# Attention state per head: row and column halves on TensorE, and float64 conversions spread over the chunks

## Chip, cores and metric

One kernel runs on one core of a Trainium2 chip. The metric is the time of an execution on the device, in microseconds (us); lower is better. Engines are called by the names of the profile: PE (TensorE, matmul), PEld (its weight loads), DVE (VectorE), ACT (ScalarE), POOL (GpSimd) and SP (SyncE, which here issues DMA transfers).

## What is computed

Three parts, one after the other. The kernel also takes the weights of the last part as float64 bits.

```python
# attention, B=4, H=8, S=768, D=48
for t in range(S):
    cur = einsum('bhd,bhde->bhde', u * k[t], v[t])
    y[t] = einsum('bhd,bhde->bhe', r[t], state + cur)
    state = w[:, None] * state + einsum('bhd,bhe->bhde', k[t], v[t])
# x: 3072 tokens x 384; routing of tokens to 8 experts, 384 tokens each
logits = x @ w_gate                       # tokens are handed out in order of the largest logit
out[mask_e] = relu(x[mask_e] @ w1[e]) @ w2[e]
# final mlp, 2048 wide
h = relu(x @ w_in);  result = (h * h) @ w_out
```

## The kernel before

**Attention.** The 768 steps of each of four batch entries are cut into six chunks of 128, so there are 24 chunks; chunk n belongs to batch n % 4 and is number c = n // 4 in it. Heads are worked on in four pairs i: the even head of a pair lies on partitions 0 to 47, the odd one on 64 to 111. For each chunk PE makes the products of r and k (`qk`, into `pA`), which DVE masks into `AM` (`am`); the gate columns of v (`vw`, into `pvw`); y in `pY` (`yout`), as the sum of the state's part, r times `T`, and the part inside the chunk, `AM` times v; and the chunk's own addition to the state (`kvm`, into `pkv`). The state `T[b]` is a block matrix of 112 x 112 per pair of heads, with zeros outside the two 48 x 56 blocks. So one matmul per pair takes both heads' state, and `tput` (DVE, from c = 1 on, ACT at c = 0) writes the two blocks apart, with the decayed state from `tdecay` (ACT) added. A chunk with c = 0 has no state's part, and the last four chunks make no state. `yev` adds `cv` to y, writes it to DRAM (`xs`, `xd`), and sums the gate logits into `L`.

The loop body works on three chunks at a time: qk of n + 1, the preparation of n + 2 (`prep`, `prep_cc` on DVE, `prep_ru`, `prep_ruk`, `prep_kk` on POOL), and yout, kvm, yev, tput of n. The loads of n + 4 (`rk`, `tk`) stand at its start in SP's queue. Within the attention every engine works in the order in which the code is written. Between these operations `R.step()` drops in steps of the routing of tokens, two a chunk, three from n = 16 and four from n = 20.

**Conversion.** The weights of the final mlp, `wi` and `wo`, 16 slabs each of 128 x 384, arrive as float64, 384 KB a slab. `Resident.fetch` asks for the slabs in turn (wi 0, wo 0, wi 1, ...), at most `ahead` of them at a time, into five buffers. `Resident.convert` cuts the work on a slab into pieces: c (L848), low (L849) and join (L845) on DVE put the float32 bits together; ACT then copies them into the high part (L830) and DVE subtracts it for the low part, the finish (L825). In the attention the finish is a piece of its own. In the first routing ACT's copy and the finish follow the join at once; in the first expert they follow one and two ticks later. `fill(n)` issues n pieces, alternating between two slabs.

**After the attention.** `close0` and `route(0)` choose the first expert's tokens: three rounds of comparing (`cm`), counting on PE (`misc`), `sat` and `n`, with one piece before sat and, in the first two rounds, one before n. Six more pieces and the loads of w1 and w2 follow. Then, for each of the eight experts, `expert` multiplies by w1 and w2 (split into `wh` by ACT and `wl` by DVE), and `mlp` by wi (`gmm`) and wo (`omm`). In the first expert three pieces are issued a tick, in its mlp two; before `gmm` of a slab its conversion has to be done. In this part PE and SP keep the order of the code, and a scheduler orders DVE, ACT and POOL.

Of the kernel before, what the change touches and what calls it, by code (L numbers as in the profile page):

```python
# [25 lines left out]
FT = mybir.dt.float32  # L26
# [4 lines left out]
AF = mybir.ActivationFunctionType  # L31
OP = mybir.AluOpType
AX = mybir.AxisListType

B, H, S, D = 4, 8, 768, 48
C = 128
NC = S // C
NCH = B * NC
# [7 lines left out]
NW, NRAW = 7, 5  # L46

def make_ident(nc, ident):
    nc.gpsimd.memset(ident, 1.0)
    nc.gpsimd.affine_select(ident, ident, pattern=[[1, 128]], compare_op=OP.is_equal, fill=0.0, base=0,  # L50
                            channel_multiplier=-1)


def attention(ctx, tc, a, R, L, RW, xd):
# [5 lines left out]
    V, G, A_, PE = nc.vector, nc.gpsimd, nc.scalar, nc.tensor  # L60
    att = ctx.enter_context(tc.tile_pool(name="att", bufs=1))
    ld = ctx.enter_context(tc.tile_pool(name="ld", bufs=5))
    wk = ctx.enter_context(tc.tile_pool(name="wk", bufs=2))
    ps = ctx.enter_context(tc.tile_pool(name="aps", bufs=1, space=bass.MemoryType.PSUM))
    p0, p1 = slice(0, 48), slice(64, 112)
    bh = lambda x: x.rearrange("p h e -> p (h e)")


    RK, TK = {}, {}
# [27 lines left out]
    ident = R.ident  # L97
    hm, hm2 = att.tile([128, 3, 8], FT, name="hm"), att.tile([128, 3, 8], FT, name="hm2")
    mask = att.tile([128, 128], FT, name="mask")
    T = [att.tile([112, 4, 112], FT, name=f"T{b}") for b in range(B)]  # L100
    kkb = [att.tile([128, 4, 112], FT, name=f"kk{j}") for j in range(2)]
    V.memset(Pw[:, :, :, 0:1], 1.0)
    V.memset(Qw[:, 1, :, 8:9], 1.0)
    warm = att.tile([1, 1], FT, name="warm")
    V.memset(dense, 1.0)
    V.memset(warm, 0.0)
    lead = ps.tile([128, 512], FT, name="pY", bufs=2)
    for _ in range(26):
        PE.matmul(lead, dense[:, :128], dense, start=True, stop=True)
    A_.activation(warm, warm, AF.Copy)  # L110
    for t in T[:2]:
        V.memset(t, 0.0)
    make_ident(nc, ident)
    for t in T[2:]:
        G.memset(t, 0.0)
    G.memset(mask, 1.0)
    G.affine_select(mask, mask, pattern=[[1, 128]], compare_op=OP.is_gt, fill=0.0, base=0, channel_multiplier=-1)
    G.iota(hm, pattern=[[128, 3], [-48, 8]], base=0, channel_multiplier=1, allow_small_or_imprecise_dtypes=True)
# [60 lines left out]
    t1s, cc, cv, pA, AM, pYs, tTs, pk = ({} for _ in range(8))  # L179

    def va(n):
        return TK[n][:, 768:1216].rearrange("p (h e) -> p h e", h=8)

    def prep(n):
        V.tensor_tensor(flat(RK[n]), flat(RK[n]), flat(WRK), op=OP.mult)
# [27 lines left out]

    def qk(n):
        AM[n] = wk.tile([128, 2, 4, 128], FT, name="AM")
        pA[n] = [ps.tile([128, 4, 128], FT, name="pA", bufs=4) for _ in range(2)]
        for i in range(4):
            for s, q in enumerate((p0, p1)):
                PE.matmul(pA[n][s][:, i], RK[n][q, 1, i], RK[n][q, 0, i], start=True, stop=True)  # L219

    def am(n, s):
        V.tensor_tensor(AM[n][:, s], pA[n][s], mask[:, None, :].to_broadcast([128, 4, 128]), op=OP.mult)

    def yout(n):
        c, b = divmod(n, B)


        p = ps.tile([128, 512], FT, name="pY", bufs=2)[:, :504].rearrange("p (h e) -> p h e", e=56)
        pYs[n] = p[:, :8]
        for i in range(4):  # L230
            if c:
                PE.matmul(bh(p[:, 2 * i:2 * i + 2, :]), RK[n][:, 0, i], T[b][:, i, :], start=True, stop=True,  # L232
                          skip_group_check=True)
            for s in range(2):
                h = 2 * i + s
                PE.matmul(p[:, h::8 - h], AM[n][:, s, i], TK[n][:, 768 + 56 * h:880 + 56 * h], start=not c,  # L236
                          stop=True, skip_group_check=True)

    def yev(n):

        c, b = divmod(n, B)
        j = b * NC + c
        xs = wk.tile([128, 8, 48], FT, name="xs")
        p = pYs[n]
        end = n == NCH - 1

        def put():
            if end:
                A_.activation(xs, p[:, :, :48], AF.Copy)
                G.tensor_tensor(xs, xs, cv[n][:, :, :48], op=OP.add)  # L250
            else:
                V.tensor_tensor(xs, p[:, :, :48], cv[n][:, :, :48], op=OP.add)
            nc.sync.dma_start(xd[j * 128:(j + 1) * 128], xs.rearrange("p h d -> p (h d)"))

        if not end:
            put()
        R.step(wide=False)
        lt = wk.tile([128, 8, 8], FT, name="lt")
        V.tensor_tensor(lt, p[:, :, 48:56], cv[n][:, :, 48:56], op=OP.add)  # L259
        R.step()  # L260
        V.tensor_reduce(L[:, j, :], lt.rearrange("p h e -> p e h"), axis=AX.X, op=OP.add)
        return put


    def tdecay(n):
        c, b = divmod(n, B)
        if c in (0, NC - 1):
            return
        t = tTs[n] = wk.tile([112, 4, 112], FT, name="tT")
        for i in range(4):  # L270
            A_.activation(t[:, i], T[b][:, i], AF.Copy, scale=W128[:, i])

    def kvm(n):
        if n // B == NC - 1:
            return
        p = pk[n] = ps.tile([112, 4, 112], FT, name="pkv")
        for i in range(4):
            PE.matmul(p[:, i, :], kkb[n % 2][:, i, :], bh(va(n)[:, 2 * i:2 * i + 2, :]), start=True, stop=True)  # L278

    def tput(n, s):  # L280
        c, b = divmod(n, B)
        if c == NC - 1:
            return
        x = slice(64 * s, 64 * s + 48), slice(None), slice(56 * s, 56 * s + 56)
        if c == 0:
            A_.activation(T[b][x], pk[n][x], AF.Copy)
        else:
            V.tensor_tensor(T[b][x], pk[n][x], tTs[n][x], op=OP.add)

    def keep_clock():  # L290
        t = ps.tile([128, 384], FT, name="pvw")
# [24 lines left out]
    for n in range(NCH):  # L316
        f1, f2 = n + 1 < NCH, n + 2 < NCH
        if n + 4 < NCH:
            load(n + 4)
        R.pace(n)  # L320
        if n == NCH - B:
            R.cnt0 = ps.tile([128, 4, 112], FT, name="pkv").rearrange("p a b -> p (a b)")
        tdecay(n)
        if f1:
            prep_cv(n + 1)
            qk(n + 1)
        if f2:
            prep(n + 2)
            prep_ru(n + 2)
            prep_ruk(n + 2)  # L330
            vw(n + 2)
        R.step(wide=False)
        if n + 1 < NCH - B:
            prep_kk(n + 1)
        if f1:
            am(n + 1, 0)
        R.step(wide=False)
        if f1:
            am(n + 1, 1)
        R.step(wide=False)  # L340
        yout(n)
        kvm(n)
        R.serve()
        if n >= NCH - B:
            R.flush()
        if n >= NCH - B - 1:
            keep_clock()
        if f2:
            prep_cc(n + 2)
        R.step()  # L350
        if n >= NCH - 2:
            RW.fill(5 if n == NCH - 2 else 3)
        last = yev(n)
        R.step()
        tput(n, 0)
        R.step()
        tput(n, 1)
        R.step()
        if n == NCH - 4:
            RW.ahead = NRAW  # L360
            RW.fetch()
    R.arrive(NC - 1, NC)
    RW.ahead = 2
    R.close0(ps.tile([128, 8, 8], FT, name="pvw").rearrange("p h e -> p (h e)"),
             ps.tile([128, 512], FT, name="pY", bufs=2), last)


class Routing:
# [844 lines left out]
```

## Time and profile before

| | us |
|---|---|
| runs: median (lowest to highest) of 3 | 837.24 (836.9 to 838.81) |
| profiled execution: its own time | 837.7 |
| span from the first to the last instruction | 836.0 |
| PE busy | 791.2 (95%) |
| DVE busy | 482.7 (58%) |
| ACT busy | 398.8 (48%) |
| POOL busy | 156.8 (19%) |
| mean granted clock of PE | 0.971 of full |

The profiled execution took 1.7 us more than its span. Shares of busy time are averages over parts with different limits, so what a change is worth is read from the part in which it is made. A line of the profile names the source line, the engine, the operation, and the tiles as out<-in.

### The profile page before, as it was taken

How to read it: one execution, taken by the hardware profiler on the slowest of the kernel's cores; microseconds unless marked ns; L12 is line 12 of the kernel's file. 1: busy time of each engine (PE TensorE's matmuls, PEld its weight loads, DVE VectorE, ACT ScalarE, POOL GpSimd, SP SyncE). 2: the span in 40 equal slices, each digit the busy share in tenths (PEclk: the TensorE clock that was granted, in tenths of full speed). 3: DMA queues.
4: the chain of work that ended last, by engine and by line, in shares of the span. 5: the costliest groups of instructions: out<-in, count | busy, mean ns of one | idle time of the engine just before them, and what ended most of it. 6: DMA issues, size and time to landing. Idle time of an engine off the chain costs nothing.

```text
span 836.0 us, 15218 instructions
## 1 busy us (share of the span) xinstructions
PE 791.2 (95%) x5572; PEld 757.1 (91%) x5572; DVE 482.7 (58%) x1271; ACT 398.8 (48%) x973; POOL 156.8 (19%) x256
## 2 busy tenths in 40 slices
PE   6999998397996999999999999999999999999996
PEld 4999997277886999999999999999999999999996
DVE  7789889888998457256616642674275234324211
ACT  2565553044555336444643554265426545544453
POOL 7876651020020101010101011000101010101001
PEclk9999999599997999999999999999999999999999
DMA  8988885164344204021302220131104023102000
GB/s 242 316 271 282 278 251 178 39 199 160 115 151 162 67 2 143 1 67 35 108 1 67 68 77 27 41 94 49 58 11 142 1 78 103 29 1 67 1 1 29
DMA packets 37515, 83.78 MB, mean 100 GB/s; under 512 B 5696, under 2 KB 25280, under 8 KB 37440
## 3 DMA queue, kind: packets, MB, share of 16 engines
q1 hardware_dynamic: 34368, 73.37, 28.1%
q0 software_dynamic: 3072, 9.44, 3.3%
q8 instruction: 44, 0.72, 0.4%
q14 instruction: 31, 0.25, 0.1%
HBM read 73.35 MB, written 9.44 MB: 99 GB/s over the span
## 4 chain that ended last, share of the span: by engine, by line
PE 83%; DVE 9%; DMA 4%; ACT 2%; issue 1%; SPq 1%; POOL 0%; POOLq 0%; DVEq 0%; ACTq 0%
PE acc L911 11%; PE ph L911 11%; PE acc L913 11%; PE acc L912 11%; PE ph L912 11%; PE ph L913 11%; PE pY L236 4%; PE pA L219 2%; PE pvw L211 2%; DMA raw<-in_w_dram 2%; PE pkv L278 2%; PE pY L232 2%; PE misc L652 2%; PE ph L980 2%; DMA tk<-in_tk_dram 1%; DVE raw L845 1%
## 5 line engine op out<-in xcount | busy, mean ns | idle before, releaser
L1025 DVE TENSOR_TENSOR al<-t,ah 128x384 fp32r<-128x384 f32 x128 | 71.3, 557 | 163.8 <-ACT t L1022 163.5
L1018 ACT ACTIVATE t<-ph 128x384 f32<-128x384 f32 x128 | 62.4, 488 | 144.2 <-PE ph L913 139.7
L908 DVE TENSOR_TENSOR wl<-raw,wh 128x384 fp32r<-128x384 f32 x128 | 69.7, 554 | 79.1 <-ACT wh L907 71.3
L911 PE MATMUL ph<-YH,wi 128*128 128x384 f32 x288 | 99.2, 344 | 6.4 <-ACT wi L830 6.4
L907 ACT ACTIVATE wh<-raw 128x384 fp32r<-128x384 f32 x128 | 65.1, 521 | 76.9 <-PE ph L912 28.3
L911 PE MATMUL acc<-wo,ah 128*128 128x384 f32 x288 | 98.3, 341 | 0.0
L913 PE MATMUL ph<-YH,wi 128*128 128x384 f32 x288 | 97.4, 338 | 0.3 <-DVE wi L825 0.2
L912 PE MATMUL ph<-YL,wi 128*128 128x384 f32 x288 | 97.3, 338 | 0.0
L912 PE MATMUL acc<-wo,ah 128*128 128x384 f32 x288 | 97.2, 338 | 0.0
L913 PE MATMUL acc<-wo,al 128*128 128x384 f32 x288 | 97.1, 337 | 0.0
L1040 POOL DMA_INDIRECT out_dram<-rows,idx x24 | 25.2, 1050 | 293.8 <-ACT rows L1038 289.5
L911 PE MATMUL acc<-ah,wh 128*128 128x384 f32 x192 | 67.1, 350 | 4.6 <-ACT wh L907 4.6
L1022 ACT ACTIVATE t<-t 128x384 f32<-128x384 f32 x128 | 67.1, 524 | 2.9
L1021 ACT ACTIVATE ah<-t 128x384 fp32r<-128x384 f32 x128 | 67.1, 524 | 2.8
L206 ACT ACTIVATE cv<-tk,cc 128x56 f32<-128x56 f32 x192 | 47.0, 328 | 41.4 <-DVE lt L259 41.4
L913 PE MATMUL acc<-ah,wl 128*128 128x384 f32 x192 | 65.3, 340 | 0.4 <-DVE wl L908 0.3
L912 PE MATMUL acc<-al,wh 128*128 128x384 f32 x192 | 65.1, 339 | 0.0
L911 PEld LDWEIGHTS ph<-YH,wi 128*128 128x128 f32 x288 | 54.5, 189 | 10.2 <-ACT wi L830 7.2
L236 PE MATMUL pY<-tk,AM 128*128 128x112 f32 x384 | 58.2, 281 | 0.0
L911 PE MATMUL ph<-XH,wh 128*128 128x384 f32 x168 | 57.0, 339 | 0.0
L913 PE MATMUL ph<-XH,wl 128*128 128x384 f32 x168 | 56.2, 335 | 0.0
L912 PE MATMUL ph<-XL,wh 128*128 128x384 f32 x168 | 56.1, 334 | 0.0
(241 smaller groups left out, 1808.7 us busy)
## 6 DMA issues: line engine op xcount, KB each, us to landing
raw<-in_w_dram SPq DMA_DIRECT2D x128, 192.0 KB, 2.5
tk<-in_tk_dram SPq DMA_DIRECT2D x24, 800.0 KB, 6.4
rk<-in_rk_dram SPq DMA_DIRECT2D x24, 448.0 KB, 6.2
raw<-in_wi_dram SPq DMA_DIRECT2D x16, 384.0 KB, 3.3
raw<-in_wo_dram SPq DMA_DIRECT2D x16, 384.0 KB, 3.2
xd<-xs SPq DMA_DIRECT2D x24, 192.0 KB, 2.2
rows<-xd,idx POOLq DMA_INDIRECT x24
out_dram<-rows,idx POOLq DMA_INDIRECT x24
```

What stands on the lines that cost most here:

```text
L206: A_.activation(cv[n][:, h], va(n)[:, h], AF.Copy, scale=cc[n][:, h:h + 1])
L236: PE.matmul(p[:, h::8 - h], AM[n][:, s, i], TK[n][:, 768 + 56 * h:880 + 56 * h], start=not c, stop=True, skip_group_check=True)
L907: A_.activation(hi, t, AF.Copy)
L908: (eng or V).tensor_tensor(lo, t, hi.bitcast(FT), op=OP.subtract)
L911: PE.matmul(o, l[0], r[0], start=first, stop=False)
L912: PE.matmul(o, l[0], r[1], start=False, stop=False)
L913: PE.matmul(o, l[1], r[0], start=False, stop=last)
L1018: A_.activation(t, o, AF.Relu)
L1021: A_.activation(gh, t, AF.Square)
L1022: A_.activation(t, t, AF.Square)
L1025: later(2, lambda: V.tensor_tensor(gl, t, gh.bitcast(FT), op=OP.subtract))
L1040: h = G.indirect_dma_start(out=out, out_offset=bass.IndirectOffsetOnAxis(ap=st[p]["idx"][:, i:i + 1], axis=0), in_=t, in_offset=None)
```

## The change

T becomes 56 wide: for each pair i the even head's 48 x 56 block on the lower partitions and the odd head's on the upper, with a fifth, zero entry behind the four. The state's part of y moves out of `yout` into a new `yinter`, called right after qk of the next chunk: eight matmuls of 48 rows, the even heads on the lower row half of the array and into one PSUM bank, the odd heads on the upper half and into another. Each writes 2 x 56 columns, of which the second 56 fall into an unused column block. `yout` then adds to what stands there. `kvm` makes each head's addition with a matmul of its own, the even head on columns 0 to 63 of the array, the odd one on 64 to 111, each with 56 columns of v. `tput` is one instruction. pY takes four PSUM banks instead of two, and pA two instead of four. Of the conversion, one piece is issued in each chunk from n = 9 to 21, four in chunk 22 and three in 23 (before: five and three, and none earlier); slabs are asked for from chunk 7 on. Access patterns of `yev` and the tiles of the lead matmuls and of `close0` follow from this. The diff, without these:

```diff
--- before.py
+++ after.py
...
-    T = [att.tile([112, 4, 112], FT, name=f"T{b}") for b in range(B)]
+    T = [att.tile([112, 5, 56], FT, name=f"T{b}") for b in range(B)]
...
-    lead = ps.tile([128, 512], FT, name="pY", bufs=2)
+    lead = ps.tile([128, 512], FT, name="pvw")
...
-    for t in T[:2]:
-        V.memset(t, 0.0)
     make_ident(nc, ident)
-    for t in T[2:]:
-        G.memset(t, 0.0)
+    for t in T:
+        G.memset(t[:, 4], 0.0)
...
     def qk(n):
         AM[n] = wk.tile([128, 2, 4, 128], FT, name="AM")
-        pA[n] = [ps.tile([128, 4, 128], FT, name="pA", bufs=4) for _ in range(2)]
+        pA[n] = [ps.tile([128, 4, 128], FT, name="pA", bufs=2) for _ in range(2)]
...
+    def yinter(n):
+        c, b = divmod(n, B)
+        p = ps.tile([128, 2, 512], FT, name="pY", bufs=2)[:, :, :504].rearrange("p s (i e) -> p s i e", e=56)
+        pYs[n] = p
+        for i in range(4 if c else 0):
+            for s, q in enumerate((p0, p1)):
+                PE.matmul(p[:, s, i::8 - i], RK[n][q, 0, i], T[b][q, i:i + 2], start=i == 0, stop=True, skip_group_check=True)
+
     def yout(n):
         c, b = divmod(n, B)
-        p = ps.tile([128, 512], FT, name="pY", bufs=2)[:, :504].rearrange("p (h e) -> p h e", e=56)
-        pYs[n] = p[:, :8]
+        p = pYs[n]
         for i in range(4):
-            if c:
-                PE.matmul(bh(p[:, 2 * i:2 * i + 2, :]), RK[n][:, 0, i], T[b][:, i, :], start=True, stop=True,
-                          skip_group_check=True)
             for s in range(2):
                 h = 2 * i + s
-                PE.matmul(p[:, h::8 - h], AM[n][:, s, i], TK[n][:, 768 + 56 * h:880 + 56 * h], start=not c,
-                          stop=True, skip_group_check=True)
+                PE.matmul(p[:, s, i::8 - i], AM[n][:, s, i], TK[n][:, 768 + 56 * h:880 + 56 * h],
+                          start=not c and i == 0, stop=True, skip_group_check=True)
...
     def tdecay(n):
...
-        t = tTs[n] = wk.tile([112, 4, 112], FT, name="tT")
+        t = tTs[n] = wk.tile([112, 4, 56], FT, name="tT")
...
     def kvm(n):
...
-        p = pk[n] = ps.tile([112, 4, 112], FT, name="pkv")
+        p = pk[n] = ps.tile([112, 4, 56], FT, name="pkv")
         for i in range(4):
-            PE.matmul(p[:, i, :], kkb[n % 2][:, i, :], bh(va(n)[:, 2 * i:2 * i + 2, :]), start=True, stop=True)
-
-    def tput(n, s):
+            for s, m in enumerate((64, 48)):
+                PE.matmul(p[64 * s:64 * s + m, i, :], kkb[n % 2][:, i, 64 * s:64 * s + m], va(n)[:, 2 * i + s, :],
+                          start=True, stop=True)
+
+    def tput(n):
...
         if c == 0:
-            A_.activation(T[b][x], pk[n][x], AF.Copy)
+            A_.activation(T[b][:, :4], pk[n], AF.Copy)
         else:
-            V.tensor_tensor(T[b][x], pk[n][x], tTs[n][x], op=OP.add)
+            V.tensor_tensor(T[b][:, :4], pk[n], tTs[n], op=OP.add)
...
             qk(n + 1)
+        yinter(n)
         if f2:
...
-        if n >= NCH - 2:
-            RW.fill(5 if n == NCH - 2 else 3)
+        if n >= 9:
+            RW.fill(1 if n < NCH - 2 else 4 if n < NCH - 1 else 3)
         last = yev(n)
         R.step()
-        tput(n, 0)
+        tput(n)
         R.step()
-        tput(n, 1)
         R.step()
-        if n == NCH - 4:
-            RW.ahead = NRAW
+        if n >= 7:
+            RW.ahead = 2 if n < NCH - 4 else NRAW
             RW.fetch()
```

On PE a chunk with a state reads, before (L219 is qk, L211 vw, L232 the state's part, L236 the part from AM, L278 kvm):

```order
L219 MATMUL pA<-rk 128x128 x8
L211 MATMUL pvw<-Wx,tk 128x64 x3
L232 MATMUL pY<-T_113,rk 128x112
L236 MATMUL pY<-tk,AM 128x2x56 x2
L232 MATMUL pY<-T_113,rk 128x112
L236 MATMUL pY<-tk,AM 128x2x56 x2
L232 MATMUL pY<-T_113,rk 128x112
L236 MATMUL pY<-tk,AM 128x2x56 x2
L232 MATMUL pY<-T_113,rk 128x112
L236 MATMUL pY<-tk,AM 128x2x56
L236 MATMUL pY<-tk,AM 128x112
L278 MATMUL pkv<-tk,kk_115 112x112 x4
```

and with the change (L217 is qk, L209 vw, L232 yinter, L240 yout, L284 kvm, of which four of eight rows stand here):

```order
L217 MATMUL pA<-rk 128x128 x8
L232 MATMUL pY<-T_113,rk 128x2x56 x8
L209 MATMUL pvw<-Wx,tk 128x64 x3
L240 MATMUL pY<-tk,AM 128x2x56 x8
L284 MATMUL pkv<-tk,kk_115 64x56
L284 MATMUL pkv<-tk,kk_115 48x56
L284 MATMUL pkv<-tk,kk_115 64x56
L284 MATMUL pkv<-tk,kk_115 48x56
```

The state's part has moved from between the matmuls of yout to a place behind qk, ahead of vw, and kvm has twice as many, smaller matmuls.

On DVE in the first round of the first routing, from the last comparison on, before:

```order
L438 TENSOR_TENSOR cm<-key_188,thr 128x384
L848 TENSOR_SCALAR c_2020<-raw_1748 128x384
L679 TENSOR_SCALAR sat<-misc 128x8
L848 TENSOR_SCALAR c_2021<-raw_1750 128x384
L688 TENSOR_REDUCE n<-misc 128x1
```

and with the change (L444 is the comparison, L851 a join, L831 a finish, L685 sat, L694 n):

```order
L444 TENSOR_TENSOR cm<-key_188,thr 128x384
L851 SCALAR_TENSOR_TENSOR raw_1658<-raw_1658 128x384
L831 TENSOR_TENSOR wie_73<-raw_1658,wie_72 128x384
L685 TENSOR_SCALAR sat<-misc 128x8
L851 SCALAR_TENSOR_TENSOR raw_1660<-raw_1660 128x384
L831 TENSOR_TENSOR woe_75<-raw_1660,woe_74 128x384
L694 TENSOR_REDUCE n<-misc 128x1
```

Since the queue of pieces is further on, a join with its finish now stands where a c stood.

On DVE at the end of the conversion, in the mlp of the first expert, before (L779 is XL, the next expert's tokens; L1025 al, the low part of the mlp's middle; L620 lm):

```order
L908 TENSOR_TENSOR wl<-raw,wh 128x384
L825 TENSOR_TENSOR wo_1976<-raw_3032,wo_1975 128x384
L1025 TENSOR_TENSOR al<-t,ah 128x384
L779 TENSOR_TENSOR XL<-misc,XH 128x3x128
L848 TENSOR_SCALAR c_3143<-raw_3036 128x384
L848 TENSOR_SCALAR c_3144<-raw_3141 128x384
L849 SCALAR_TENSOR_TENSOR raw_3036<-raw_3036,c_3143 128x384
L849 SCALAR_TENSOR_TENSOR raw_3141<-raw_3141,c_3144 128x384
L845 SCALAR_TENSOR_TENSOR raw_3036<-raw_3036 128x384
L845 SCALAR_TENSOR_TENSOR raw_3141<-raw_3141 128x384
L620 TENSOR_TENSOR lm<-L,pen 128x192
L825 TENSOR_TENSOR wi_1974<-raw_3036,wi_1973 128x384
```

and with the change (L914 is wl, L854 c, L855 low, L851 join, L831 finish, L1031 al, L785 XL):

```order
L855 SCALAR_TENSOR_TENSOR raw_3064<-raw_3064,c_3164 128x384
L1031 TENSOR_TENSOR al<-t,ah 128x384
L914 TENSOR_TENSOR wl<-raw,wh 128x384
L855 SCALAR_TENSOR_TENSOR raw_3162<-raw_3162,c_3165 128x384
L851 SCALAR_TENSOR_TENSOR raw_3064<-raw_3064 128x384
L914 TENSOR_TENSOR wl<-raw,wh 128x384
L851 SCALAR_TENSOR_TENSOR raw_3162<-raw_3162 128x384
L831 TENSOR_TENSOR wi_2140<-raw_3064,wi_2139 128x384
L1031 TENSOR_TENSOR al<-t,ah 128x384
L831 TENSOR_TENSOR wo_2142<-raw_3162,wo_2141 128x384
L785 TENSOR_TENSOR XL<-misc,XH 128x3x128
```

The finish of the last wi, the lowest row before, now stands ahead of the three XL and of lm, behind 13 al and 21 wl of the first and second expert where it stood behind 15 and 23.

## Rows read from the trace of the kernel before

**Rows 1.** Windows: stretch and its us, busy us (x instructions) by engine, clock, DMA share, GB/s.

```profile
core 0: us, PE busy (x) PEld busy (x) DVE busy (x) ACT busy (x) POOL busy (x), PEclk, DMA share, GB/s
38.39:87.08 48.69, 48.69 (x487) 46.63 (x486) 43.04 (x86) 31.45 (x123) 34.68 (x37) 1.00 0.87 284
119.65:149.80 30.15, 24.73 (x244) 22.46 (x243) 28.51 (x82) 9.80 (x38) 6.08 (x5) 0.95 0.49 161
208.20:247.20 39.00, 36.21 (x272) 34.74 (x272) 37.30 (x111) 22.25 (x48) 2.52 (x10) 1.00 0.38 122
277.70:836.00 558.30, 551.72 (x3615) 541.00 (x3614) 243.47 (x650) 266.77 (x559) 53.00 (x99) 1.00 0.17 51
```

**Rows 2.** Chain of waits: start us, us, what. A chunk without state, one with.

```profile
35.85 1.83 PE pY L236 x16
...
61.19 0.81 PE pvw L211 x6
...
64.72 0.79 PE pkv L278 x8
65.51 1.09 PE pA L219 x16
```

**Rows 3.** Timeline of TensorE: start us, us, engine, line, operation, tiles, shapes.

```profile
64.47 0.87 PEld L278 LDWEIGHTS pkv<-tk,kk 128*112 128x112 f32 x8
...
139.22 0.61 PE L236 MATMUL pY<-tk,AM 128*128 128x112 f32 x4
139.76 0.42 PE L558 MATMUL pkv<-oh,cm 128*64 128x8 bf16 x8
```

**Rows 4.** Timeline of VectorE in one chunk; in brackets the idle time before.

```profile
65.67 0.78 DVE L288 TENSOR_TENSOR T<-pkv,tT 48x224 f32<-48x224 f32 x2
...
68.72 0.68 DVE L222 TENSOR_TENSOR AM<-pA,mask 128x512 f32<-128x512 f32 x1
...
70.17 0.56 DVE L252 TENSOR_TENSOR xs<-pY,cv 128x384 f32<-128x384 f32 x1 [0.31 <-PE pY L236]
```

**Rows 5.** DMA issues, 40 to 120 us: count, KB each, median us to landing.

```profile
tk<-in_tk_dram SPq DMA_DIRECT2D x14, 800.0 KB, 6.2
```

**Rows 6.** Timeline of VectorE in the first routing.

```profile
152.05 0.35 DVE L848 TENSOR_SCALAR c<-raw 128x384 int32<-128x384 int32 x1
152.62 0.17 DVE L679 TENSOR_SCALAR sat<-misc 128x8 bf16<-128x8 f32 x1 [0.22 <-PE misc L652]
152.70 0.35 DVE L848 TENSOR_SCALAR c<-raw 128x384 int32<-128x384 int32 x1
153.04 0.17 DVE L688 TENSOR_REDUCE n<-misc 128x1 f32<-128x8 f32 x1
...
159.97 0.55 DVE L845 SCALAR_TENSOR_TENSOR raw<-raw 128x384 int32<-128x384 int32 x1
161.13 0.56 DVE L825 TENSOR_TENSOR wie<-raw,wie 128x384 fp32r<-128x384 f32 x1 [0.61 <-ACT wie L830]
161.60 0.16 DVE L679 TENSOR_SCALAR sat<-misc 128x8 bf16<-128x8 f32 x1
```

**Rows 7.** Timeline of VectorE: the last pair of slabs converted, in the first expert.

```profile
264.50 0.62 DVE L848 TENSOR_SCALAR c<-raw 128x384 int32<-128x384 int32 x2
265.04 1.02 DVE L849 SCALAR_TENSOR_TENSOR raw<-raw,c 128x384 int32<-128x384 int32 x2
265.98 1.02 DVE L845 SCALAR_TENSOR_TENSOR raw<-raw 128x384 int32<-128x384 int32 x2
...
267.18 0.55 DVE L825 TENSOR_TENSOR wi<-raw,wi 128x384 fp32r<-128x384 f32 x1
```

**Rows 8.** Waits, 174 to 278 us: us in total, times, longest us.

```profile
PE ph L911 <- ACT wi L830: 6.4, 3, 3.7
...
PE acc L911 <- ACT wh L907: 4.6, 3, 2.3
```

**Rows 9.** Windows in which TensorE's clock was half, columns as in rows 1.

```profile
259.20:262.60 3.40, 3.40 (x13) 3.30 (x12) 2.73 (x7) 2.62 (x6) 0.00 (x0) 0.50 0.60 179
266.10:272.80 6.70, 5.63 (x18) 5.51 (x19) 6.48 (x20) 2.56 (x5) 0.00 (x0) 0.50 0.00 1
```

**Rows 10.** Chain of waits at the start of the kernel.

```profile
6.91 12.36 DMA tk<-in_tk_dram
```

More of the change, by code (lines that the diff above doesn't have):

```diff
@@ L243, in yev @@
         xs = wk.tile([128, 8, 48], FT, name="xs")
-        p = pYs[n]
+        by_half = lambda x: x.rearrange("p (i s) d -> p s i d", s=2)
+        p = pYs[n][:, :, :4]
         end = n == NCH - 1
@@ L248, in put @@
             if end:
-                A_.activation(xs, p[:, :, :48], AF.Copy)
+                A_.activation(by_half(xs), p[..., :48], AF.Copy)
                 G.tensor_tensor(xs, xs, cv[n][:, :, :48], op=OP.add)
             else:
-                V.tensor_tensor(xs, p[:, :, :48], cv[n][:, :, :48], op=OP.add)
+                V.tensor_tensor(by_half(xs), p[..., :48], by_half(cv[n][:, :, :48]), op=OP.add)
             nc.sync.dma_start(xd[j * 128:(j + 1) * 128], xs.rearrange("p h d -> p (h d)"))
@@ L258, in yev @@
         lt = wk.tile([128, 8, 8], FT, name="lt")
-        V.tensor_tensor(lt, p[:, :, 48:56], cv[n][:, :, 48:56], op=OP.add)
+        V.tensor_tensor(by_half(lt), p[..., 48:56], by_half(cv[n][:, :, 48:56]), op=OP.add)
         R.step()
@@ L283, in tput @@
             return
-        x = slice(64 * s, 64 * s + 48), slice(None), slice(56 * s, 56 * s + 56)
         if c == 0:
-            A_.activation(T[b][x], pk[n][x], AF.Copy)
+            A_.activation(T[b][:, :4], pk[n], AF.Copy)
         else:
-            V.tensor_tensor(T[b][x], pk[n][x], tTs[n][x], op=OP.add)
+            V.tensor_tensor(T[b][:, :4], pk[n], tTs[n], op=OP.add)
     def keep_clock():
@@ L364, in attention @@
     R.close0(ps.tile([128, 8, 8], FT, name="pvw").rearrange("p h e -> p (h e)"),
-             ps.tile([128, 512], FT, name="pY", bufs=2), last)
+             ps.tile([128, 4, 128], FT, name="pA", bufs=2).rearrange("p i t -> p (i t)"), last)
 class Routing:
```

## The prediction

> **What bounds the kernel now.** I read the stretches first. The attention part runs from about 25 to 150 us. Until 119.65 TensorE is busy all of the time (48.69 of 48.69 us, VectorE 43.04); from there to 149.80 VectorE is (28.51 of 30.15, TensorE 24.73). From about 174 to 277.70 the first of the eight experts runs, and VectorE is the fullest again: 37.30 of 39.00 us between 208.20 and 247.20. From 277.70 on TensorE is busy 551.72 of 558.30 us, and the change touches nothing there [rows 1].
>
> The chain of waits gives a chunk's price on TensorE. In a chunk with a state it goes round in 5.41 us: qk 1.09 (L219), vw 0.81 (L211), both parts of y 2.72 (61.19 + 0.81 to 64.72), kvm 0.79 (L278). The part of y from AM alone takes 1.83 for 16 instructions, 0.114 each, so the state's part (8 instructions) is 0.89 [rows 2]. An fp32 matmul is two instructions in these rows.
>
> Of the waits of TensorE in the first expert, the two that matter are on wi conversions (6.4 us in 3 waits, the longest 3.7) and on the split of w (4.6 in 3) [rows 8].
>
> **The change, part by part.** The sum is made against the profiled execution, 837.7 us; the median of the runs shown is 0.5 lower.
>
> *State's part of y (yinter).* Four matmuls with 112 rows become eight with 48 rows, in pairs on the two row halves and two PSUM banks. qk already does just this: 16 instructions of 128 columns in 1.09, which is 0.136 a pair with its surroundings, against 0.114 for one full-height instruction [rows 2]. Eight pairs at 0.114 are 0.91 against 0.89 now: **0**. They stand right behind qk, so they add no change between halves and full height. If pairs did not overlap it would be +0.9 a chunk; the qk row excludes that.
>
> *States (kvm).* Four matmuls on 112 columns become eight, on 64 and 48 columns, in pairs on the two column halves. An instruction takes 0.114 with 128 stationary columns and 0.79/8 = 0.099 with 112 [rows 2], so about 0.88 ns a column. Pairs that overlap: 8 x 64 x 0.88 ns = 0.45, a gain of 0.34. Pairs one after the other: 8 x (64 + 48) x 0.88 ns = 0.79, no gain. No row shows two column halves at once; the nearest is qk with its row halves, which overlap, so I take 0.45. Against this stands one more change of the array's shape a chunk. The rows price such changes three times: qk has 1.09 - 8 x 0.114 = 0.18 over its pairs, vw has 0.81 - 6 x 0.114 = 0.13 [rows 2], and L558, on 64 columns, starts 0.09 later than the next instruction in step would (139.22 + 4 x 0.112 = 139.67, it starts at 139.76) [rows 3]. I take 0.15. Together -0.19 a chunk, between -0.25 and +0.18. It counts for chunks in which TensorE is the bound, 0 to 18; I leave out the last three, in which routing steps grow on VectorE: 16 x -0.19 = **-3.0** (-4.8 to +3.4).
>
> *VectorE in a chunk.* tput falls from two instructions (0.78) to one of about 0.4. From chunk 9 each chunk gets one conversion piece: two pieces of each of the four kinds in eight chunks, 0.27 for a c and 0.47 for the others [rows 7], 0.42 on average. VectorE's round is now 5.41 less 0.31 idle = 5.10 [rows 4]; it becomes 4.70 in the early chunks and 5.12 from chunk 9, still under TensorE's 5.22. **0** while that cover of 0.1 holds; without it, each 0.1 over costs 0.9 for nine chunks.
>
> *The added wait.* pA has two buffers instead of four, so qk of the next chunk waits until both AM halves are read. The second ends at 69.40 and the next qk starts at 65.51 + 5.41 = 70.92 [rows 2, 4]: 1.5 us early. Behind that wait on TensorE stand yinter, vw and yout, and xs on VectorE waits for yout. **0**.
>
> *DMA.* Four slabs of 384 KB move to chunks 7 and 9, in SP's queue between the loads of two chunks; their buffers are free, so nothing behind them waits in the queue. At 284 GB/s a pair takes 2.8 us, and the DMA engines have 13% spare, 0.7 us a chunk [rows 1]; the backlog peaks at 2 x 2.8 - 2 x 0.7 = 4.2. A load is issued two chunks (10.8 us) before it is read and lands after 6.2 [rows 5]: 4.6 to spare. **0**, barely; beyond it POOL's product, then cc on VectorE would be late, by a microsecond once or twice.
>
> *Last chunks, VectorE bound (19 to 23).* Five extra pieces before the two old groups (8, now 7 pieces of other kinds): chunk 19 +0.47 - 0.40, chunks 20 and 21 +0.47 each, chunk 22 (join, two finishes, c for two c, two lows, join) -0.27, chunk 23 (c, two lows for join and two finishes with a wait on ScalarE) about -0.4: **+0.3**.
>
> *First routing (150 to 163 us).* Its five filler pieces are now join, join, c, c, low where they were c, c, low, low, join. Here a join drags ScalarE's copy and the finish along: 161.60 - 159.97 = 1.63 until sat, where a c costs 152.62 - 152.05 = 0.57 [rows 6]. First +1.06, second 1.63 + 0.08 - 0.42 = +1.29, third and fourth within 0.1 and of opposite sign, fifth 0.5 for 1.63 = -1.1. **+1.2**, all on the path.
>
> *First expert.* At its start VectorE still has 28 c, 28 low, 29 join and 29 finish to do; after the change 24, 25, 26 and 26. That is 4 x 0.27 + 9 x 0.47 = 5.3 us less [rows 7]. The scheduler also puts the finish of the last wi ahead of two al, two wl, three XL and one lm that stand before it now: 7 x 0.47 + 0.27 = 3.6. So the last wi, which VectorE finishes at 267.7, comes some 8.9 earlier if VectorE keeps its small idle time. TensorE's last stall goes with it, and the half clock from 266.1 to 272.8, in which 5.63 us of matmuls ran, gives back 2.8 [rows 9]: 11.7. The other way round: the wi waits 6.4 [rows 8], plus half of 3.40 and 5.63 at the low clock [rows 9], is 10.9. I take **-11**. The lower bound is the removed VectorE work alone, -5.3. The upper one adds to 10.9 the waits on wh and the low clock behind them, in part also later loads: -17. What is late next is the split of w (4.6): its loads stand in SP's queue behind slabs that wait for conversions.
>
> Removed memsets and the new tile of the 26 lead matmuls lie before 19.3 us, under the load of tk that the chain waits for there (6.91 + 12.36) [rows 10]: 0.
>
> Sum: -3.0 + 0.3 + 1.2 - 11 = -12.5; 837.7 becomes 825.2, and **825** beside the median of 837.24.
>
> **Rivals.**
>
> *Column halves take turns.* Both halves use all rows of the array. The load of kvm's next weights does start under the running matmul (64.47 against 64.72) [rows 2, 3], but into the same 112 columns, so nothing shows two loads at once. Then kvm stays at 0.79 and only the change of shape is paid: 19 x 0.15 = +2.9 instead of -3.0, **831**. For it speaks that qk's halves split the rows, which these do not. The Trainium skill has a rule for it (TensorE: Matmul & The Clock Gate, What overlaps and what doesn't): a weight load overlaps running matmuls only when its row group differs. By that rule this rival holds; the same page's measured gain for column tiles (2.38 times with three) speaks for the forecast.
>
> *Only the work goes.* VectorE's queue shrinks by 5.3 us, but the wi finishes still arrive one by one behind other waits (XH, wh), and a half clock remains: -5.3, so -6.8 in all, **831**. For it: VectorE was 96% busy between 208 and 247 [rows 1]. Against: pieces stop earlier.
>
> *Also the w loads come free.* The waits on wh (4.6) [rows 8] and the low clock behind them go as well: -17, **819**.
>
> *Slower: narrow matmuls cost as full ones.* If each of kvm's 16 instructions takes the 0.114 of a full-width one, in turn, kvm is 1.82 + 0.15 instead of 0.79: +1.18, for 19 chunks +22, **850**. It decides from 0.5 a chunk on (9.5 saved elsewhere over 19 chunks). Against it: 112 columns already go faster than 128 [rows 2], and L558 runs eight 64-column instructions in 0.42 [rows 3].
>
> **How the numbers follow.** Forecast 0.50; halves in turn 0.18; only the work 0.18; w loads too 0.07; slower 0.07. 0.2% (1.7 us) is about what a measurement of this kernel tells from no change. Halves in turn and only the work together would give 837, no change, which I count as 0.04 out of the two. Range: 819 takes in the freed w loads, 833 the two middle rivals with 2 us of DMA or VectorE delay. Faster 0.89, same 0.04, slower 0.07.
>
> **What would show it.** Right: a chunk's round near 5.2, kvm near 0.45; sat about 1.1 later than its c-filled form; no wait on a wi conversion above 1 us in the first expert, and full clock from its mlp to the end. Wrong: kvm at 0.79 or more; VectorE without idle time before xs in chunks 9 to 18; TensorE waiting for AM before qk; or the stalls on wi still there after 250 us.

## The result and the profile after

827.74 us against 837.13: ratio 0.988, 95% interval [0.9858, 0.9902]. The same kernel timed once more beside other runs of the kernel before gave 824.92 against 837.03, 0.9848 [0.9825, 0.987]. The forecast was 825, the range 819 to 833. The profiled execution has a span of 826.9 us, 9.1 less than before.

Windows of the changed kernel, columns as in [rows 1]: chunks 2 to 19, each counted from its qk on TensorE to the next chunk's; in them the one long stretch; the routing from its first `sat` to its fourth; the first expert; the rest, but for the last 0.39 us of the span.

```profile
26.02:123.06 97.04, 94.56 (x1214) 89.21 (x1214) 80.37 (x161) 55.43 (x232) 72.09 (x73) 0.96 0.97 293
81.27:91.58 10.31, 8.01 (x73) 7.56 (x70) 5.39 (x12) 3.25 (x14) 3.89 (x5) 0.67 1.04 276
150.95:165.68 14.73, 4.07 (x76) 2.88 (x76) 12.63 (x51) 1.09 (x2) 0.30 (x2) 0.50 0.09 27
177.93:268.56 90.63, 82.61 (x548) 78.13 (x548) 84.75 (x223) 51.78 (x111) 5.36 (x18) 1.00 0.46 148
268.56:826.50 557.94, 551.76 (x3615) 541.02 (x3614) 243.43 (x650) 267.46 (x559) 53.02 (x99) 1.00 0.17 51
```

The same stretches of the kernel before, with the same marks at their ends:

```profile
24.84:119.65 94.81, 94.81 (x950) 90.59 (x950) 83.13 (x167) 59.84 (x234) 68.28 (x73) 1.00 0.88 286
147.97:161.60 13.63, 4.08 (x76) 2.88 (x76) 12.07 (x49) 0.54 (x1) 0.46 (x3) 0.50 0.01 1
174.26:277.69 103.43, 89.02 (x548) 83.61 (x549) 90.46 (x236) 52.98 (x114) 6.27 (x19) 0.93 0.45 146
```

Stage by stage, after less before: to the start of chunk 2 +1.18; chunks 2 to 19 +2.23; the last three chunks 0.00; to the first `sat` -0.43; routing +1.10; to the first expert -0.41; first expert -12.80; the other seven experts 0. The sum is -9.1. In this pair of traces the first expert gave more than forecast, and the chunks lost where they should have gained.

The chain of waits of the changed kernel, one chunk with a state and the start of the next:

```profile
49.85 1.09 PE pA L217 x16
50.95 0.88 PE pY L232 x16
51.83 0.81 PE pvw L209 x6
52.64 1.83 PE pY L240 x16
54.47 0.60 PE pkv L284 x14
55.07 1.09 PE pA L217 x16
```

A chunk goes round in 5.21 us instead of 5.41 [rows 2]. yinter takes 0.88 where the state's part took 0.89, kvm 0.60 where it took 0.79; all of the gain is kvm's. (Two of kvm's 16 records are missing here.) Where, then, do +2.23 come from? Rows of TensorE's timeline:

```profile
72.85 0.85 PE L209 MATMUL pvw<-Wx,tk 128*128 128x64 f32 x6 [0.18 <-DMA tk<-in_tk_dram]
...
78.75 1.99 PE L240 MATMUL pY<-tk,AM 128*128 128x112 f32 x16
80.67 0.67 PE L284 MATMUL pkv<-tk,kk 128*64 128x56 f32 x16
...
85.62 1.51 PE L209 MATMUL pvw<-Wx,tk 128*128 128x64 f32 x6 [2.30 <-DMA tk<-in_tk_dram]
86.92 3.70 PE L240 MATMUL pY<-tk,AM 128*128 128x112 f32 x16
90.55 1.10 PE L284 MATMUL pkv<-tk,kk 128*64 128x56 f32 x16
```

In the loop body of chunk 12 vw, which works two chunks ahead, waits 2.30 us for a tk load. While TensorE waits its clock falls to the half level (at 84.8 us), and yout then takes 3.70, where it took 1.99 in the body ahead, kvm 1.10 instead of 0.67: 10.31 us for the round, 5.10 more than its neighbours. Without that the 18 chunks come to 2.23 - 5.10 = -2.87. Two rounds earlier vw had already waited 0.18, for the load behind the first pair. The chain shows how the load came late; the second DMA row is the load that TensorE waited for:

```profile
62.24 10.47 DMA tk<-in_tk_dram
...
72.73 0.03 SPq L81
...
72.80 12.68 DMA tk<-in_tk_dram
85.48 0.14 issue
```

Before, a tk load landed after 6.2 us [rows 5]. The one issued right behind the first pair of slabs (60.68 and 61.16) took 10.47, the one issued after both pairs 12.68. The first had also been what SP waited for, 1.1 us, before it could issue the second (L81). From the first pair's issue to the wait the DMA engines had no time to spare. The second row is a like stretch of a run below, early conversions without halves, which had no such wait:

```profile
60.70:85.50 24.80, 22.44 (x308) 21.11 (x306) 21.53 (x46) 14.22 (x60) 13.53 (x14) 0.99 1.01 290
61.60:86.60 25.00, 25.00 (x254) 23.96 (x253) 24.18 (x50) 15.73 (x65) 14.75 (x18) 1.00 0.97 323
```

Busy all the time, they moved 290 GB/s, hardly more than the 284 at a share of 0.87 before [rows 1].

TensorE's waits in the first expert, after, but for those on `sat` (2.5, before 2.7) and on a comparison (0.2):

```profile
PE ph L918 <- DVE YL L1010: 1.6, 2, 0.8
PE acc L917 <- ACT wh L913: 1.5, 1, 1.5
PE acc L919 <- DVE wl L914: 1.3, 1, 1.3
PE misc L783 <- DVE XL L785: 0.7, 1, 0.7
```

No wait on a wi conversion is left (6.4 before), that on wh is 1.5 instead of 4.6 [rows 8], and the clock is full throughout. TensorE's 548 matmuls take 82.61 us at full clock; before they took 89.02. So of the 12.80, 6.41 is clock and 6.39 idle time. Before, the clock was half in the two stretches of [rows 9] and in a third, behind two waits on wh:

```profile
204.60:208.00 3.40, 3.40 (x12) 3.34 (x11) 2.47 (x6) 1.40 (x3) 0.15 (x1) 0.50 0.32 126
```

The pair of traces shows the first expert's gain on its large side. With no piece moved it takes 103.42, 102.18 and 100.74 us in three traces of this study, with the same twelve moved 90.63 to 92.52 in six. Three of those six still have 3.4 us of half clock, behind a wait on wh of 1.5 that the others have too.

In the first routing VectorE's timeline is as forecast: the join with ScalarE's copy now lies before the second and third `sat`.

```profile
155.03 0.55 DVE L851 SCALAR_TENSOR_TENSOR raw<-raw 128x384 int32<-128x384 int32 x1
156.19 0.56 DVE L831 TENSOR_TENSOR wie<-raw,wie 128x384 fp32r<-128x384 f32 x1 [0.61 <-ACT wie L836]
156.66 0.16 DVE L685 TENSOR_SCALAR sat<-misc 128x8 bf16<-128x8 f32 x1
```

### The profile page after: what moved, and what is told of

It is laid out like the page before. It is cut to its first block, busy times and chain, and to the rows that moved or that the text cites. A ratio compares the mean times of both kernels' runs of the same rounds, so it can differ in the third digit from the quotient of the medians.

```text
span 826.9 us, 15824 instructions
## 1 busy us (share of the span) xinstructions
PE 786.2 (95%) x5892; PEld 752.0 (91%) x5892; DVE 473.6 (57%) x1253; ACT 394.5 (48%) x969; POOL 160.6 (19%) x258
## 4 chain that ended last, share of the span: by engine, by line
PE 81%; DVE 8%; DMA 6%; issue 1%; POOL 1%; ACT 1%; SPq 1%; POOLq 0%; ACTq 0%
PE acc L917 11%; PE ph L917 11%; PE ph L918 11%; PE acc L918 11%; PE acc L919 11%; PE ph L919 11%; DMA tk<-in_tk_dram 4%; PE pY L240 4%; PE pA L217 2%; PE pvw L209 2%; PE misc L658 2%; DMA raw<-in_w_dram 2%; PE ph L986 2%; PE pkv L284 1%; PE pY L232 1%
## 5 line engine op out<-in xcount | busy, mean ns | idle before, releaser
L1031 DVE TENSOR_TENSOR al<-t,ah 128x384 fp32r<-128x384 f32 x128 | 71.2, 557 | 163.8 <-ACT t L1028 162.6
L914 DVE TENSOR_TENSOR wl<-raw,wh 128x384 fp32r<-128x384 f32 x128 | 69.6, 554 | 73.9 <-ACT wh L913 66.7
L917 PE MATMUL acc<-wo,ah 128*128 128x384 f32 x288 | 97.1, 337 | 0.0
L918 PE MATMUL acc<-wo,ah 128*128 128x384 f32 x288 | 96.2, 334 | 0.0
L918 PEld LDWEIGHTS ph<-YL,wi 128*128 128x128 f32 x288 | 54.1, 188 | 0.0
```

The costliest lines, as they stand in the source:

```text
L914: (eng or V).tensor_tensor(lo, t, hi.bitcast(FT), op=OP.subtract)
L917: PE.matmul(o, l[0], r[0], start=first, stop=False)
L918: PE.matmul(o, l[0], r[1], start=False, stop=False)
L1031: later(2, lambda: V.tensor_tensor(gl, t, gh.bitcast(FT), op=OP.subtract))
```

## Experiments

### The parts apart

**Halves without early conversions.** The conversions go back where they were.

```diff
-        if n >= 9:
-            RW.fill(1 if n < NCH - 2 else 4 if n < NCH - 1 else 3)
+        if n >= NCH - 2:
+            RW.fill(5 if n == NCH - 2 else 3)
...
-        if n >= 7:
-            RW.ahead = 2 if n < NCH - 4 else NRAW
+        if n == NCH - 4:
+            RW.ahead = NRAW
```

> The changed kernel with the conversions back where they were (no piece before chunk 22, slabs loaded from chunk 20 on); the row and column halves stay. Theory A (the four slabs that were moved into chunks 7 and 9 are what made the load of tk late at 85.62 us): no wait of TensorE on a tk load after the first chunks; every chunk with a state 5.21 us instead of 5.41, 16 x -0.2 = -3.2; first expert as before, 103 us; in all 837.1 - 3.2 = 834, within 1.5. Theory B (a chunk of 5.21 us is by itself too short for its own 1.47 MB of loads): TensorE waits on tk in the middle of the attention part here too, with a stretch at half clock behind it; 836 to 839.

Measured: 831.56, ratio 0.9933 [0.9908, 0.9957]. Chunks 2 to 19 take 91.37 us, 3.44 less than before, each with a state 5.21 up to chunk 18. No wait of TensorE on tk stands in its trace between 40 and 120 us, where a tk load lands after 6.3 (median; before 6.2). Theory A holds, B falls. The kernel is 2.4 faster than expected: the way from the last chunk to the first expert is 1.5 shorter, and the first expert, at 102.18, is 1.2 shorter.

**Early conversions without halves.** In the kernel before, the reverse of the diff above.

> The kernel before with only the new schedule of conversions (one piece a chunk from the tenth chunk on, slabs from chunk 7 on). Theory A: the slabs' backlog is the same, but a chunk of 5.41 us drains 0.2 us more, five chunks 1.0, so the wait on tk (2.30 in the changed kernel) becomes 1.3 or goes; first expert 90.7 us instead of 103.4 and first routing 1.1 later: 837.1 - 12.8 + 1.1 = 825.4 without a wait, up to 829.5 with one and its half clock. Theory B: no wait on tk, 825.4. If the first expert's gain needs the faster chunks too, it stays above 95 us and the time above 830.

Measured: 828.46, ratio 0.989 [0.9865, 0.9915]. No wait on tk; all chunks with a state at 5.41 until chunk 19. First expert 90.81: its gain doesn't need the faster chunks. The time is 3 above the 825.4 of a run without a wait, in its parts: start of chunk 2 +1.06, chunks 2 to 19 +0.45, the last three +0.39; and the kernel before ran 1.0 higher beside it. The slowest tk load whose landing the trace has took 8.8 us, with 10.8 in two chunks. So the same four slabs did no harm at 5.41 us a chunk. That the chunk's length alone decides is not shown: over the 25 us from the first pair on, the DMA engines moved 323 GB/s here and 315 in the next run, against 290 and 302 in the two traces of the changed kernel, at a busy share of 0.97 to 1.01 in all four. Why they moved more here stays open.

**Column halves one after the other.**

```diff
-        for i in range(4):
-            for s, m in enumerate((64, 48)):
+        for s, m in enumerate((64, 48)):
+            for i in range(4):
```

> The changed kernel with the states' matmuls issued for all four head pairs on the first column half, then all four on the second, instead of alternating. If alternating column halves run side by side (in the trace two streams, one instruction each 0.050 and 0.058 us), the grouped order takes 8 x 0.050 + 8 x 0.058 + 0.15 = 1.01 us instead of 0.60: +0.4 a chunk, +7 in all, less what of the wait on tk goes: 831 to 835. If the gain comes only from the narrower moving operand and the order does not matter: 0.60 and 827.7.

Measured: 827.94, ratio 0.9888 [0.9865, 0.9912], the time of the changed kernel, for a reason that neither theory had. kvm takes 0.81, midway between 0.60 and 1.01, and the chunk 5.41:

```profile
75.51 1.82 PE pY L240 x16
77.33 0.81 PE pkv L284 x16
78.14 1.09 PE pA L217 x16
```

The single starts show why not 1.01. The first half's eight instructions start every 58 ns up to 77.713, but the second half's begin at 77.545, when three of the first half have not started yet, and go on every 49 ns. So a part of the two halves runs side by side even in this order. And why the time didn't move: at 5.41 a chunk the wait on tk is gone. The 18 chunks lost 0.2 each and won back the 5.1 of the wait, 1.60 less in all; the first expert, with 3.4 us of half clock, took 0.75 more.

**Slabs one at a time.**

```diff
-        if n >= 7:
-            RW.ahead = 2 if n < NCH - 4 else NRAW
+        if n >= 5:
+            RW.ahead = (n >= 5) + (n >= 7) if n < 8 else (n >= 11) + (n >= 14) if n < NCH - 4 else NRAW
```

> The changed kernel with its first four slabs loaded one at a time, in chunks 5, 7, 11 and 14, instead of two in chunk 7 and two in chunk 9; the conversions stay where they are. Theory A: the backlog never exceeds one slab (1.4 us) plus the rest of the one before, under the 4.6 us of slack; the wait on tk and the half clock behind it go, -5.1: 822.6, within 1.5. Theory B: the wait stays, at the same or another chunk: 827 to 828.

Measured: 823.22, ratio 0.9827 [0.9804, 0.9849]; no wait on tk, chunks 2 to 19 again 91.37. Theory A, with its number. One slab, too, makes the tk load behind it land later, after 8.9 us (issued at 50.81), but that is within the two chunks (10.4). This is the change without its fault.

### How firm, and how much of it is needed

**The change once more**, unaltered.

> The changed kernel once more, unaltered. If the wait on tk belongs to the slabs' place in the queue, the trace again has TensorE waiting 1 to 3 us on a tk load around 85 us with a half clock behind it (chunk of 9 to 11 us), and the median stays at 826 to 829. If it was an accident of one execution, all chunks take 5.2 us and the time is 823 to 824. Also open: the 1.2 us by which its first chunks were later than those of the kernel before (half clock from 13 instead of 16 us); if that is chance, the third chunk starts anywhere from 24.8 to 26.2.

Measured: 824.92, 1 below the range that went with a wait. The wait is there again, in the same chunk and nearly as long:

```profile
63.62 10.26 DMA tk<-in_tk_dram
...
73.97 12.37 DMA tk<-in_tk_dram
86.33 0.14 issue
86.47 0.85 PE pvw L209 x6
```

This time the clock stayed full (vw 0.85), and the chunk took 7.23: the wait costs 2.0, with the half clock behind it 5.1. Chunk 2 started at 27.76. Over the 13 traces of this study it starts anywhere from 24.48 to 27.76, with nearly the same work ahead of it (the kernel before and its two variants at 24.84, 25.90 and 26.31). So the kernel before was on the early side, and the +1.18 is within chance.

**Only the first pair early.**

```diff
-        if n >= 9:
-            RW.fill(1 if n < NCH - 2 else 4 if n < NCH - 1 else 3)
+        if 9 <= n < 17 or n >= NCH - 2:
+            RW.fill(1 if n < 17 else 5 if n < NCH - 1 else 3)
...
-        if n >= 7:
-            RW.ahead = 2 if n < NCH - 4 else NRAW
+        if n >= 5:
+            RW.ahead = (n >= 5) + (n >= 7) if n < 8 else 0 if n < NCH - 4 else NRAW
```

> The changed kernel with only the first pair of slabs converted early (loaded in chunks 5 and 7, its eight pieces in chunks 9 to 16), then the old 5 and 3 pieces in the last two chunks. 8 of the 12 pieces stay moved. The first expert takes 102.2 us with none moved and 90.6 with 12. Theory of work alone (linear): 102.2 - 8 x 0.97 = 94.5. Theory of a just-in-time chain (each wi is late by what VectorE is behind; the last wait goes first): two of the three waits on wi and both half clocks go, one wait under 1 us stays or none: 91 to 93. The pieces beside the first routing are then c, c, low, low, join as before, so the routing from first to fourth sat is 13.6, not 14.7. In all 822 to 825.

Measured: 826.24, ratio 0.987 [0.9853, 0.9886]; routing 13.63 as expected, but the first expert 98.49, above both theories. Its waits on conversions and splits, and its window:

```profile
PE acc L917 <- ACT wh L913: 3.8, 3, 2.6
PE ph L917 <- ACT wi L836: 2.4, 1, 2.4
```

```profile
169.19:267.68 98.49, 88.95 (x547) 83.98 (x548) 87.02 (x228) 51.95 (x112) 5.35 (x18) 0.91 0.45 140
```

With none, 8 and 12 pieces moved, the waits on wi are 5.4, 2.4 and 0, those on wh 3.9, 3.8 and 1.5, and the matmuls take 89.70, 88.95 and 82.61 us. Eight pieces thus buy 3.7 us, about their own work (two c at 0.27 and six others at 0.47 make 3.4). The last four buy 7.9: with them the two waits fall behind which the clock is half here, from 194.5 to 204.7 behind that on wh, and from 256.0 to 262.6 around that on wi. With the spread of the traces above, 3.7 stands for 2 to 5 and 7.9 for 6 to 8; fourteen pieces (next run) bring 90.35, next to nothing more. So the gain is no straight line, but a step between eight and twelve pieces; where in between it lies was not tried, and for eight there is one trace.

**From chunk 7 on.**

```diff
-        if n >= 9:
+        if n >= 7:
...
-        if n >= 7:
-            RW.ahead = 2 if n < NCH - 4 else NRAW
+        if n >= 3:
+            RW.ahead = (n >= 3) + (n >= 5) if n < 6 else (n >= 9) + (n >= 12) if n < 13 else 0 if n < NCH - 4 else NRAW
```

> An attempt at a faster kernel: one piece a chunk already from chunk 7 on, slabs one at a time in chunks 3, 5, 9 and 12, the third pair only in chunk 20. Two more pieces (0.9 us) leave the first expert, and the pieces beside the first routing become two finishes, c, c, low, so no join with ScalarE's copy lies there: routing 13.7 instead of 14.7, first expert 0 to 1 less. 823.2 - 1.0 - 0.5 = 821.7. Against it: the DMA engines are at 1.0 of their time between 25 and 45 us too, so slabs in chunks 3 and 5 may make a tk load late (a wait of 1 to 2 us with half clock behind it, then 825).

Measured: 820.33, ratio 0.9804 [0.9788, 0.982]. Routing 12.50 (13.7 expected), first expert 90.35, no wait on tk. The last three chunks went up to 17.59, from 15.93 in the kernel without early conversions.

**Column halves alone, in the kernel before.**

```diff
-            PE.matmul(p[:, i, :], kkb[n % 2][:, i, :], bh(va(n)[:, 2 * i:2 * i + 2, :]), start=True, stop=True)
+            for s, m in enumerate((64, 48)):
+                PE.matmul(p[64 * s:64 * s + m, i, 56 * s:56 * s + 56], kkb[n % 2][:, i, 64 * s:64 * s + m],
+                          va(n)[:, 2 * i + s, :], start=True, stop=True)
```

> The kernel before with one part of the change alone: the states' matmuls in column halves (writing the diagonal blocks that are used); the state's part of y, T, the PSUM buffers and the conversions stay as before. If the column halves carry all of the chunk's gain: kvm 0.60, a chunk with a state 5.22 instead of 5.41, 18 x 0.19 = 3.4, 837.6 - 3.4 = 834. If the row halves of the state's part give or take something: 5.15 or 5.3. The kernel with both halves and no early pieces gained 6.5 (831.6), 3.0 of it behind the chunks (last chunk to the first routing 0.9, before the first expert 0.6, in it 1.2): if that comes from the other buffers, this one stays at 834; if it follows from the chunks' end alone, it shows here too, 831.5.

Measured: 832.97, ratio 0.9956 [0.9939, 0.9972]. kvm 0.60 and 5.22 to 5.23 a chunk:

```profile
59.67 0.60 PE pkv L279 x14
```

The column halves carry the chunk's gain; the row halves of y are worth 0.01. Of the 4.7 us between the two profiled spans (831.3 and 836.0), 2.7 lies in the first expert (100.74 against 103.42) with the same conversions in it, which no part of this change explains. From the last chunk to the first `sat` it takes 12.15 and from the fourth `sat` to the first expert 12.66, as before (12.16, 12.66). With the row halves and their buffers these are 11.25 and 12.09 (first run above), so those 1.5 us belong to the other half of the change. What in it brings them was not tried.

### Pairs, and a try at a faster kernel

**The second pair in chunk 13** instead of 9.

```diff
-            RW.ahead = 2 if n < NCH - 4 else NRAW
+            RW.ahead = 2 if n < 8 else 0 if n < 13 else 2 if n < NCH - 4 else NRAW
```

> The changed kernel with its slabs still loaded two at a time, but the second pair in chunk 13 instead of 9. If the wait on tk at 85.6 us comes from four slabs within 7 us (5.5 us of transfers against 4.6 of slack), two at once (2.8) stay under it: no wait, every chunk with a state at 5.21, 823 to 824. If two slabs side by side are already too much, a wait of about 1 us comes some four chunks behind each pair: 825 to 828.

Measured: 825.97, ratio 0.9869 [0.9847, 0.989]. No long wait, but three short ones in TensorE's timeline, none behind the first pair, all behind the later ones:

```profile
103.13 0.85 PE L209 MATMUL pvw<-Wx,tk 128*128 128x64 f32 x6 [0.31 <-DMA tk<-in_tk_dram]
108.76 0.85 PE L209 MATMUL pvw<-Wx,tk 128*128 128x64 f32 x6 [0.38 <-DMA tk<-in_tk_dram]
125.69 0.85 PE L209 MATMUL pvw<-Wx,tk 128*128 128x64 f32 x6 [0.33 <-DMA tk<-in_tk_dram]
```

Both theories were too simple: behind the second pair a tk load takes 10.72 us, a little more than two chunks of 5.21. That no wait came behind the first pair and three behind the later ones may be because the later ones found the first not yet worked off: the DMA engines' share stays at 1.03 to 1.04 from 70 to 90 us. That was not tried apart. The three waits are 1.0 us together. One slab at a time is the form without such a wait, in all five traces that load the first slabs so.

**Two pieces each in chunks 7 and 8, none in 20 and 21** (22 pieces in all, slabs in chunks 3, 5, 8 and 10).

```diff
-        if n >= 9:
-            RW.fill(1 if n < NCH - 2 else 4 if n < NCH - 1 else 3)
+        if 7 <= n < NCH - 4 or n >= NCH - 2:
+            RW.fill(2 if n < 9 else 1 if n < NCH - 2 else 4 if n < NCH - 1 else 3)
...
-        if n >= 7:
-            RW.ahead = 2 if n < NCH - 4 else NRAW
+        if n >= 3:
+            RW.ahead = (n >= 3) + (n >= 5) if n < 6 else (n >= 8) + (n >= 10) if n < 12 else 0 if n < NCH - 4 else NRAW
```

> An attempt to beat the kernel that converts from chunk 7 on (820.3): the same 22 pieces, but two each in chunks 7 and 8, where VectorE has 0.9 to 1.1 us to spare, and none in chunks 20 and 21, where that kernel lost 1.6 us (last three chunks 17.6 instead of 15.9); slabs in chunks 3, 5, 8 and 10. Expected 820.3 - 1.6 = 818.7, within 1. Against it: 0.94 us for two pieces in chunk 8 with VectorE's 4.3 is 5.24, just over TensorE's 5.21; and the slab in chunk 8 comes three chunks behind the one in 5.

Beside it the kernel from chunk 7 on, once more:

> The kernel that converts from chunk 7 on, once more, on the same chip as the attempt to beat it: 820 to 821.5.

Measured: 821.1, ratio 0.9824 [0.9802, 0.9845], and 821.99, ratio 0.9837 [0.9811, 0.9864]: no difference that can be told, and the 818.7 was missed. The last three chunks take 16.93 against 17.20, not 15.93. Both medians lie below the 827.74 and 824.92 of the changed kernel, but their intervals overlap that of its second measurement ([0.9825, 0.987]), as does the 0.9827 with slabs one at a time. Only the first measurement from chunk 7 on, 0.9804 [0.9788, 0.982], lies clear of both.

## Why the prediction was right, and where it was off

- **Sign and size.** Forecast -12.5, measured -9.1 in the profiled execution; with the chance at the start taken off, about -10.3. It came as near as that partly by luck: +5.1 from DMA and +1.2 at the start stand against -1.8 in the first expert and -1.1 in the last chunks and the ways to and from the routing.
- **kvm and yinter.** Right: kvm 0.45 + 0.15 against 0.60 measured (eight starts 58 ns apart are 0.46), yinter 0.91 against 0.88, -0.19 a chunk against -0.20. "Halves in turn" falls: kvm would be 0.79 or more, and the grouped order shows the second half starting before the first is through. By the rule of the Trainium skill that stood with that rival (TensorE: Matmul & The Clock Gate, What overlaps and what doesn't) it would have held; the traces decide otherwise for column halves, with 0.60 against 0.79. "Slower" falls with it.
- **The step that failed: DMA, "0, barely".** The sum had 2 x 2.8 us of slabs, less 2 x 0.7 drained, against 4.6 of slack. The 13% spare was no spare: with the slabs in the queue the DMA engines were busy at 1.01 and still moved only 290 GB/s, so next to nothing drained between the pairs. The slack was 4.2: two rounds of 5.21, not 5.41, less 6.2. And a pair adds 4.1 to 4.5 to a tk load's landing (10.26, 10.47 and 10.72 against 6.2), not 2.8; behind both pairs it was 12.37 and 12.68, and SP issued that load late because an earlier one had not landed. Why a pair costs more than its transfer stays open. The price of going over was not POOL's product late "by a microsecond once or twice" but a wait of TensorE itself, whose vw reads tk, of 2.0 to 2.3, with a half clock behind it in one of two traces: +2.0 to +5.1.
- **VectorE's cover.** It held for TensorE: chunks at 5.21, but for the long one, one at 5.43 with the wait of 0.18 on tk, and the last at 5.41, which it takes without the pieces too. The sign that I had named against it did come, no idle time of VectorE before xs in most chunks from 75.7 us on, and cost TensorE nothing. The pieces cost more than I had priced them (next section but one). The wait for pA, forecast at 0, is 0 in the changed kernel; in the one-slab kernel and the last two it is 0.4 to 0.5 once, at the qk of chunk 22, where VectorE is late.
- **Last chunks.** From the start of chunk 20 to the first `sat` the five traces with the changed kernel's pieces take 27.52 to 29.25, the one without them 27.18: +0.3 to +2.1, and 0.7 in the first trace of the change, against +0.3.
- **First routing.** +1.10 between the first and fourth `sat` against +1.2.
- **First expert.** -12.8 against -11, and -8.2 to -12.8 over the traces with none and with twelve pieces moved. The waits on wi (6.4) went, as said. Half clock back: 6.4, where I had 2.8 to 4.5; half of the third stretch (204.60 to 208.00), which my upper figure left out, is 1.7 of it. The wait on wh, which I had put into a rival of 0.07, fell by 3.1, and new waits on wl, YL and XL (3.6) took that back. "Only the work goes" falls: 5.3 us of work brought 8.2 at the least. Its price fits a part of the way, though, the first eight pieces.

## What to carry to other kernels

Work that is moved under a busy stretch brings its loads along. Add the transfers to that stretch's own demand, at its new, shorter length, and bring them one at a time where the share of the DMA engines is near 1; idle time of those engines is no promise of bytes, as 0.87 gave 284 GB/s here and 1.01 gave 290. Work taken from the engine that feeds TensorE paid in a step here: pieces were worth their own time until the waits went behind which the clock fell, and then several times that.

## What was not expected of the hardware

A conversion piece beside a product on POOL takes longer. In the kernel with slabs one at a time, the same instruction on VectorE twice, and POOL's:

```profile
123.23 1.36 DVE L855 SCALAR_TENSOR_TENSOR raw<-raw,c 128x384 int32<-128x384 int32 x1
...
129.74 0.55 DVE L855 SCALAR_TENSOR_TENSOR raw<-raw,c 128x384 int32<-128x384 int32 x1
```

```profile
123.18 1.00 POOL L187 TENSOR_TENSOR t<-tk,U 128x384 f32<-128x384 f32 x1 [4.89 <-DMA tk<-in_tk_dram]
124.26 1.20 POOL L190 TENSOR_TENSOR t<-t,tk 128x384 f32<-128x384 f32 x1
127.11 0.99 POOL L187 TENSOR_TENSOR t<-tk,U 128x384 f32<-128x384 f32 x1 [1.65 <-DVE rk L183]
128.18 1.00 POOL L190 TENSOR_TENSOR t<-t,tk 128x384 f32<-128x384 f32 x1
```

The first lies beside POOL's two products and takes 0.81 more; the second lies clear of it. In the 13 traces the two-operand pieces without POOL beside them never took over 0.58, while beside POOL's products several took 0.80 to 1.37 (others no more than alone). I had priced the pieces from the first expert [rows 7], where POOL does little; how much of the last chunks' growth this makes was not tried apart. The Trainium skill (SBUF — State Buffer, SBUF: two separate sides) says that an instruction of VectorE with two inputs in SBUF and one of GpSimd that reads SBUF lock each other out; the rows agree, with 1.36 against 0.55.

Two instructions on different column halves do not keep the order of issue: the second half's first started 0.17 us ahead of the first half's last (77.545 against 77.713).
